# An MLP's first product as three float32r products of split operands, in place of a seven-product float32 scheme

## The chip, the cores and the metric

The kernel runs on one core of a Trainium2 chip. The metric is the device time of one execution in microseconds. The core has five engines that run side by side and wait for each other by semaphores: TensorE (PE in the profile; its weight loads are listed apart as PEld), VectorE (DVE), ScalarE (ACT), GpSimd (POOL) and SyncE (SP), which issues the transfers.

## The reference

An mLSTM cell is followed by an MLP with exact Gelu. The cell is a recurrence over 768 steps, for 4 batches and 8 heads of width 40. Its output, 3072 tokens by 320, is the MLP's input.

```python
for t in range(S):                                   # S = 768
    m_new = np.maximum(f_gate[:, :, t] + m, i_gate[:, :, t])
    f_stab = np.exp(f_gate[:, :, t] + m - m_new)
    i_stab = np.exp(i_gate[:, :, t] - m_new)
    C = f_stab * C + i_stab * (v k^T)                # cut: written with einsum
    n = f_stab * n + i_stab * k
    y[:, :, t] = sigmoid(o_gate) * (C q) / max(|n . q|, 1)
...
x = attn_out.transpose(0, 2, 1, 3).reshape(B * S, H * D)   # 3072 x 320
h = x @ w_in                                         # Up:   320 -> 2048
g = 0.5 * h * (1.0 + erf(h * inv_sqrt2))             # Gelu
return (g @ w_out).astype(np.float32)                # Down: 2048 -> 320
```

The weights w_in and w_out come as 64-bit floats; the kernel turns them into float32 on the chip.

## The kernel before

The sequence is cut into six chunks of 128 steps. In a chunk the four batches give 512 tokens (TG = 512), and the work has three parts: the cell in its chunked form (scores, carried state, values), Up with Gelu, and Down. The cell's work for the next chunk is woven into Down of the present one. The order of all steps is written as strings of letters, such as DOWN below: T is the turning (transposing) of k and q, W the weights exp(a - M), S the scores, C the carried state, V the values, Y the finish of the cell's output, X its turning, F a step of Down, M the masking of a loaded tile, G the output gate, Z a sum of weights.

```python
DOWN = """
    M0 Z M1 T0 W0 F F T1 W1 Z G3 Z F S0 Z S1 C0 M2 Z C1 G1 G0 M3 V0 Y0 Z V1 W2 Z F F T2 W3 F T3 F G2 Z Y1 S2 S3 C2
    V2 C3 Y2 V3 F F Y3 X0 F F X1 X2 F F X3 F"""
```

Up of the first chunk is a plain float32 product. For chunks two to six the kernel cuts the 320 rows of x into two blocks of 128 and a rest of 64. On the two blocks it uses a scheme of seven block products where the plain way has eight, with sums of weight blocks (in_sums, made once) and of x blocks (x_sums, made in every chunk). The rest of 64 rows is done as half-row products: two of them lie on the two halves of the array.

```python
def sum_x():                                         # once per chunk, on VectorE
    (b11, b12), (b21, b22) = x_blocks()
    t1, t2, t4 = x_sums
    for to, x, y in ((t1, b12, b11), (t2, b22, t1), (b12, b22, b12), (t4, b21, t2)):
        nc.vector.tensor_tensor(out=to, in0=x, in1=y, op=OP.subtract)

def summed_up(g, sums_too):
    ...
    def product(to, lhs, rhs, f0, first, last):
        for j in range(2):                           # 128 x 128 weights, 256 columns of x
            nc.tensor.matmul(to[:, j, :], lhs[:, (f0 + j) * P:(f0 + j + 1) * P], rhs, ...)      # L597

    def products(f0, to_sum):
        ...
        product(c11, a11, b11, f0, True, False)
        nc.scalar.copy(out=blk[1][1], in_=c11)                                                  # L606
        product(c12, s2, t2, f0, True, True)
        nc.vector.tensor_tensor(out=blk[0][0], in0=c12, in1=blk[1][1], op=OP.add)               # L608
        product(c21, s1, t1, f0, True, True)
        nc.vector.tensor_tensor(out=blk[0][1], in0=c21, in1=blk[0][0], op=OP.add)               # L610
        product(c22, s3, t3, f0, True, False)
        nc.vector.tensor_tensor(out=blk[1][0], in0=c22, in1=blk[0][0], op=OP.add)               # L612
        ...                                          # sums of hidden blocks for Down
        product(c11, a12, b21, f0, False, False)
        product(c12, s4, b22, f0, True, False)
        product(c21, a22, t4, f0, True, False)

    def rest(f0, pair, h):
        for j in range(2):
            for e in range(2):                       # e: half of the array's rows
                nc.tensor.matmul(pair[e][:, j, :], w_rest[halves[e], ...], xT[halves[e], NX, ...], ...)  # L626

    for group in ((0, 2), (4, 6)):
        sets = [products(f, group[0]) for f in group]
        ...                                          # rest for each half of the tokens
        # Gelu of c11 from PSUM (L637); the other three: add in VectorE (L639), then Gelu (L640)
    hidden_sums(g, HF - 4, HF)
```

Down uses a seven-product scheme as well (the F steps, L682), with sums of the hidden blocks (hidden_sums) and of w_out (weight_sum). Neither is changed.

The buffers that the change touches: q, k and v have four each, the mask tile Mb two and the weights W four; w_in and the sums lie in tiles of their own.

```python
qb = [const.tile([P, H, DP], F32, name=f"qb{n}") for n in range(NLD)]      # NLD = 4; kb, vb likewise
...
Mb[n] = wts.tile([P, H, L], F32, name="Mb", tag="Mb", bufs=NM)             # NM = 2
...
W[n] = wts.tile([P, H, L], F32, name="W", tag="W")                         # 4 buffers
...
# turn_y, the turning of the cell's output:
nc.scalar.copy(out=xT[:, :, t], in_=px)
if self.c > 0:
    load(n + NLD)                                    # q, k, v, o_gate of the batch four ahead
```

Of the kernel before, what the change touches and what calls it, by code (L numbers as in the profile page):

```python
# [9 lines left out]
F32 = mybir.dt.float32  # L10
BF16 = mybir.dt.bfloat16
# [4 lines left out]
P = 128  # L16

I23 = 2.0 ** 23

# [8 lines left out]
    K K J T0 W0 O6 M2 O7 A J W1 S0 C0 K J T1 L7 U U K Z K V0 T2 A M3 J J G1 S1 K W2 W3 K C1 Z A S2 Z V1 G2 J Y0 J K  # L28
    C2 Z T3 J K Y1 U U J S3 Z V2 C3 K J K K J J F K F F F Z J K J X0 K K J F F F Z J F K G3 Y2 F J K V3 J K F K X1 J
    J F F F F K Z X2 B8 J F Y3 X3 B9 F"""  # L30
DOWN = """
    M0 Z M1 T0 W0 F F T1 W1 Z G3 Z F S0 Z S1 C0 M2 Z C1 G1 G0 M3 V0 Y0 Z V1 W2 Z F F T2 W3 F T3 F G2 Z Y1 S2 S3 C2
    V2 C3 Y2 V3 F F Y3 X0 F F X1 X2 F F X3 F"""
# [3 lines left out]
def kernel(  # L37
# [32 lines left out]
    NM = 2  # L70
    NB = 4
    WP = 512
    assert S % L == 0 and 3 * BH <= P and DFF % (4 * WP) == 0 and DM == NX * P + R and DM <= WP and D <= DP and NLD == B == 4

    const = ctx.enter_context(tc.tile_pool(name="const", bufs=1))
    wts = ctx.enter_context(tc.tile_pool(name="wts", bufs=B))
# [14 lines left out]

    w_in = const.tile([P, NX, 2, DFF // 2], F32, name="w_in")
    w_rest = const.tile([P, DFF // 2], F32, name="w_rest")
# [4 lines left out]
    xT = const.tile([P, NX + 1, TG], F32, name="xT")  # L98
# [5 lines left out]
    qb = [const.tile([P, H, DP], F32, name=f"qb{n}") for n in range(NLD)]  # L104
    kb = [const.tile([P, H, DP], F32, name=f"kb{n}") for n in range(NLD)]
    vb = [const.tile([P, H, D1], F32, name=f"vb{n}") for n in range(NLD)]

    ob = [const.tile([P, DM + R], F32, name=f"ob{n}") for n in range(NLD)]
# [7 lines left out]
    def out_of(n):  # L116
        return ob[n % NLD][:, 0:DM].rearrange("p (h d) -> p h d", d=D)

    def load(n, first=0, end=4):

        if n >= NCH * B:
            return
        c, b = divmod(n, B)
        for src, dst in ((q, qb), (k, kb), (v, vb), (o_gate, None))[first:end]:
            nc.sync.dma_start(out=dst[n % NLD][:, :, 0:D] if dst else out_of(n),
                              in_=src[b, :, c * L:(c + 1) * L, :].rearrange("h p d -> p h d"))

    Mb, W = {}, {}

    def load_M(n):  # L130

        if n >= NCH * B:
            return
        c, b = divmod(n, B)
        Mb[n] = wts.tile([P, H, L], F32, name="Mb", tag="Mb", bufs=NM)
        nc.sync.dma_start(out=Mb[n].rearrange("p h l -> p (h l)"),
                      in_=M_d[c - 1, b * H:(b + 1) * H, :].rearrange("h l -> (h l)").unsqueeze(0).to_broadcast([P, H * L]))
# [3 lines left out]
    for t in kb[0:B] + qb[0:B]:  # L141
        nc.gpsimd.memset(t[:, :, D:DP], 0.0)
    for t in vb[0:B]:
        nc.gpsimd.memset(t[:, :, D:D1], 1.0)
# [19 lines left out]
    M_left = gates.tile([BH, 2, L], F32, name="M_left")  # L164
# [85 lines left out]
    w_cols = lambda e, f, n: slice(DFF * e + 2 * f, DFF * e + 2 * (f + n))  # L250
    for f in range(0, DFF // 2, WP // 2):
        for x in range(NX):
            pieces.append(([w_src["in"][x * P:(x + 1) * P, w_cols(e, f, WP // 2)] for e in range(2)],
                           w_in[:, x, :, f:f + WP // 2]))
        if f % WP == 0:
            pieces.append(([w_src["in"][NX * P:DM, w_cols(e, f, WP)] for e in range(2)], w_rest[:, f:f + WP]))
    n_in = len(pieces)
# [34 lines left out]
    def conv_two(i):  # L292

        if i < len(pieces):
# [5 lines left out]
            if len(dst.shape) == 3:  # L300
                s, p = [t.rearrange("p (e f) -> p e f", e=2) for t in (s, p)]
# [20 lines left out]
    class Cell:  # L322


        def __init__(self, c):
# [3 lines left out]
            self.qT, self.kT, self.vw, self.far, self.hs = {}, {}, {}, {}, {}  # L329
# [7 lines left out]
        def weights(self, b):  # L337

            n = self.c * B + b
            W[n] = wts.tile([P, H, L], F32, name="W", tag="W")  # L340
            if self.c > 0:
                M_n = Mb.pop(n)
# [17 lines left out]
            if self.c > 0 and not 2 * B <= n + NM < 2 * B + NM:  # L360
                load_M(n + NM)

        def gate(self, b):
            o = ob[(self.c * B + b) % NLD][:, 0:DM]
            nc.scalar.activation(out=o, in_=o, func=AF.Sigmoid)

        def turn(self, b):
            n = self.c * B + b
            for src, store, name in ((kb, self.kT, "kT"), (qb, self.qT, "qT")):
                pt = ps_tr.tile([P, NP, L], F32, name="pt", tag="tr")  # L370
                unread(pt[:, 0, :])
                for p in range(NP):
                    nc.tensor.transpose(pt[:, p, :], src[n % NLD][:, 2 * p:2 * p + 2, :].rearrange("p h d -> p (h d)"),  # L373
# [6 lines left out]
        def weigh_values(self, b):  # L380
            vw = self.vw[b] = two.tile([P, H, D1], F32, name="vw", tag="vw")
            self.engine.tensor_tensor(out=vw, in0=vb[(self.c * B + b) % NLD],
# [17 lines left out]
        def carry(self, b):  # L400
# [9 lines left out]
            if c + 1 < NCH:  # L410
                vw = self.vw.pop(b)
                for p in range(NP):
                    for hip in range(2):
                        nc.tensor.matmul(pc[halves[hip], p, :], kb[n % NLD][:, 2 * p + hip, :], vw[:, 2 * p + hip, :],  # L414
                                         start=True, stop=True)
            if c > 0:
# [4 lines left out]
                self.far[b] = two.tile([P, H, D1], F32, name="far", tag="far")  # L421
# [12 lines left out]

        def values(self, b):
# [6 lines left out]
            for h in range(H):  # L442
                for r in halves:
                    nc.tensor.matmul(ph[r, h, :], Pm[:, h, r], vb[n % NLD][:, h, :], start=True, stop=True)  # L444
# [3 lines left out]
            hs = self.hs[b] = two.tile([P, H, D1], F32, name="hs", tag="hs")  # L448
            nc.vector.tensor_tensor(out=hs, in0=ph, in1=self.far.pop(b), op=OP.add)

        def finish(self, b):
            n, hs = self.c * B + b, self.hs.pop(b)
            ys, y = ob[n % NLD], out_of(n)
            self.engine.tensor_tensor(out=y, in0=hs[:, :, 0:D], in1=y, op=OP.mult)
            den = two.tile([P, H], F32, name="den", tag="den")
# [4 lines left out]
            nc.vector.tensor_copy(out=ys[:, DM:DM + R], in_=ys[:, DM - R:DM])  # L460

        def turn_y(self, b):
# [6 lines left out]
            for k in range(NX + 1):  # L469
                nc.tensor.transpose(px[:, k, :], ob[n % NLD][:, k * P:(k + 1) * P], ident)  # L470
            nc.scalar.copy(out=xT[:, :, t], in_=px)  # L471
            if self.c > 0:
                load(n + NLD)
            if self.c > 0 and b == B - 1:
                sum_x()
# [12 lines left out]
    w_sums, in_sums, x_sums = [], [], []  # L488
    T = {1: lambda j: w_sums[0][:, j, :], 2: lambda j: w_sums[1][:, j, :], 3: Bm[0][1]}

    def sums_begin():

        gate_ctx.close()
        pool = ctx.enter_context(tc.tile_pool(name="sums_of", bufs=1))
        w_sums.extend(pool.tile([P, HF, HD], F32, name=f"w_sums{n}") for n in range(2))
        in_sums.extend(pool.tile([P, DFF // 2], F32, name=f"in_sums{n}") for n in range(3))
        x_sums.extend(pool.tile([P, HT], F32, name=f"x_sums{n}") for n in range(3))
# [31 lines left out]
    def up_step(g, sets):  # L529

        banks = []
        for k, (i0, i1, t0, t1) in sets:
            banks.append([ps_mm.tile([P, i1 - i0, t1 - t0], F32, name="pu", tag="ab"[k % 2]) for e in range(2)])
            for e in range(2):

                for i in range(i0, i1):
                    for x in range(NX):
                        nc.tensor.matmul(banks[-1][e][:, i - i0, :], w_in[:, x, e, i * P:(i + 1) * P], xT[:, x, t0:t1],  # L538
                                         start=(x == 0 and i == i0), stop=False, skip_group_check=True)
        for pu, (_, (i0, i1, t0, t1)) in zip(banks, sets):  # L540
            for i in range(i0, i1):
                for e in range(2):
                    r = halves[e]
                    nc.tensor.matmul(pu[e][:, i - i0, :], w_rest[r, i * P:(i + 1) * P], xT[r, NX, t0:t1], start=False,  # L544
                                     stop=(i + 1 == i1), skip_group_check=True)
# [26 lines left out]
    def in_sum(i):  # L572
        f, (a11, a12), (a21, a22) = slice(WP * (i // 4), WP * (i // 4 + 1)), *[[w_in[:, x, e, :] for x in range(NX)]
                                                                               for e in range(2)]
        s1, s2, s4 = in_sums
        to, x, y, op = ((s1, a21, a22, OP.add), (s2, s1, a11, OP.subtract), (a21, a11, a21, OP.subtract),
                        (s4, a12, s2, OP.subtract))[i % 4]
        nc.vector.tensor_tensor(out=to[:, f], in0=x[:, f], in1=y[:, f], op=op)

    def x_blocks():  # L580
        return [[xT[:, x, HT * h:HT * (h + 1)] for h in range(2)] for x in range(NX)]

    def sum_x():
        (b11, b12), (b21, b22) = x_blocks()
        t1, t2, t4 = x_sums
        for to, x, y in ((t1, b12, b11), (t2, b22, t1), (b12, b22, b12), (t4, b21, t2)):
            nc.vector.tensor_tensor(out=to, in0=x, in1=y, op=OP.subtract)

    def summed_up(g, sums_too):
        (a11, s3), (a12, a22) = [[w_in[:, x, e, :] for e in range(2)] for x in range(NX)]  # L590
        s1, s2, s4 = in_sums
        (b11, t3), (b21, b22) = x_blocks()
        t1, t2, t4 = x_sums
        def product(to, lhs, rhs, f0, first, last):

            for j in range(2):
                nc.tensor.matmul(to[:, j, :], lhs[:, (f0 + j) * P:(f0 + j + 1) * P], rhs, start=(first and j == 0),  # L597
                                 stop=(last and j == 1), skip_group_check=True)

        def products(f0, to_sum):  # L600

            blk = [[g.t[:, HF * e + f0:HF * e + f0 + 2, HT * h:HT * (h + 1)] for h in range(2)] for e in range(2)]
            c11, c12, c21, c22 = [pool.tile([P, 2, HT], F32, name="pu", tag=tag)
                                  for pool, tag in ((ps_tr, "tr"), (ps_h, "h"), (ps_mm, "a"), (ps_mm, "b"))]
            product(c11, a11, b11, f0, True, False)
            nc.scalar.copy(out=blk[1][1], in_=c11)  # L606
            product(c12, s2, t2, f0, True, True)
            nc.vector.tensor_tensor(out=blk[0][0], in0=c12, in1=blk[1][1], op=OP.add)  # L608
            product(c21, s1, t1, f0, True, True)
            nc.vector.tensor_tensor(out=blk[0][1], in0=c21, in1=blk[0][0], op=OP.add)  # L610
# [188 lines left out]
```

## Time and profile before

| | |
|---|---|
| time, median of three runs | 518.1 us |
| span of the profiled execution | 515.2 us |
| span until the second chunk's Up begins | 133.2 us |
| from one Up to the next (chunks three to five) | 79.6 us |
| Down of the last chunk | 30.6 us |
| transfers | 41.6 MB, mean 81 GB/s |
| mask tile Mb, 512 KB: issue to landing, median | 3.7 us |
| q, k, v, 160 KB each: issue to landing, median | 4.0, 4.5, 4.9 us |

How to read the lines. A group line has the source line, the engine and operation, output<-input, shapes, the count, then the busy time and the mean length of one, then the idle time of the engine before them with what ended most of it. A matmul's length is its latency; matmuls overlap, so their spacing is read from the chain or from the stages. The chain is the work that ended last, followed back from the end: each line is its start, its length and what it was. A stage line has the busy time of each engine in a stretch, the number of instructions in brackets, then the granted TensorE clock, the share of the transfer engines and their GB/s.

### The profile page before, as it was taken

Reading aid. Unit: us, or ns where it says so; the run is one execution under the profiler, and the core shown is the slowest. Engines: PE = TensorE matmul, PEld = TensorE weight load, DVE = VectorE, ACT = ScalarE, POOL = GpSimd, SP = SyncE. Lnnn points to the kernel's source line nnn. Section 1 sums busy time; section 2 is a strip of 40 time slices with the busy share of each in tenths; the row PEclk is TensorE's granted clock in tenths of the full one; section 3 lists DMA queues with packets and bytes.
Section 4 is the critical chain, followed back from the end, with each engine's and each line's share of the span. In section 5 each row is a group of like instructions: output and inputs, shape, how many; then the busy total and the mean of one; then the engine's idle time right before and its main releaser. Section 6 shows DMA issues by size and latency. Waiting matters only on the chain.

```text
span 515.2 us, 10957 instructions
## 1 busy us (share of the span) xinstructions
PE 500.3 (97%) x4472; PEld 450.6 (87%) x4472; DVE 340.2 (66%) x696; ACT 255.0 (49%) x523; POOL 60.9 (12%) x98
## 2 busy tenths in 40 slices
PE   4889999999999999999999999999999999999997
PEld 3778888767888999988999988999988999988997
DVE  7789598999577887347668347678347657237621
ACT  7696999555344960152980132982123882124300
POOL 3002100000210225000145000053000021000000
PEclk9799999999999999999999999999999999999999
DMA  6999751279900254900234900124920020000001
GB/s 128 223 214 212 184 147 53 64 163 171 198 0 1 84 116 58 167 0 2 74 88 69 167 28 1 43 83 81 166 52 2 5 80 1 27 27 0 1 2 51
DMA packets 111442, 41.62 MB, mean 81 GB/s; under 512 B 101184, under 2 KB 104416, under 8 KB 111392
## 3 DMA queue, kind: packets, MB, share of 16 engines
q1 hardware_dynamic: 111392, 40.92, 37.5%
q8 instruction: 35, 0.57, 0.5%
q14 instruction: 15, 0.12, 0.1%
HBM read 36.90 MB, written 4.01 MB: 79 GB/s over the span
## 4 chain that ended last, share of the span: by engine, by line
PE 91%; ACT 4%; DVE 3%; issue 0%; DMA 0%; SPq 0%; DVEq 0%; ACTq 0%
PE po L682 30%; PE pu L597 24%; PE pu L626 7%; PE po L659 7%; PE pu L538 5%; PE ps L395 4%; PE ph L444 4%; PE pt L373 4%; PE pf L419 2%; PE pf L414 2%; PE pu L544 1%; PE px L470 1%; ACT W L359 1%; ACT pow L285 1%; ACT pow L286 1%; DVE M L194 1%
## 5 line engine op out<-in xcount | busy, mean ns | idle before, releaser
L682 PE MATMUL po<-w_out,g 128*128 128x160 f32 x640 | 91.5, 299 | 0.0
L682 PEld LDWEIGHTS po<-w_out,g 128*128 128x128 f32 x640 | 88.0, 190 | 0.3 <-DVE g L639 0.3
L597 PE MATMUL pu<-xT,w_in 128*128 128x256 f32 x240 | 58.8, 381 | 0.0
L639 DVE TENSOR_TENSOR g<-pu,g 128x512 f32<-128x512 f32 x60 | 40.5, 689 | 22.4 <-PE pu L626 21.0
L597 PEld LDWEIGHTS pu<-xT,w_in 128*128 128x128 f32 x240 | 45.0, 190 | 7.5 <-ACT g L640 1.7
L471 ACT COPY xT<-px 128x384 f32<-128x384 f32 x24 | 11.1, 480 | 77.9 <-PE px L470 77.8
L359 ACT ACTIVATE W<-Mb,aT 128x128 f32<-128x128 f32 x160 | 48.9, 391 | 0.1
L682 PE MATMUL po<-w_sums,sums 128*128 128x160 f32 x320 | 47.3, 302 | 0.0
L398 DVE TENSOR_TENSOR W<-ps,W 128x512 f32<-128x512 f32 x48 | 30.2, 683 | 23.9 <-PE ps L395 21.2
L334 POOL TENSOR_SCALAR_AFFINE_SELECT Mb<-Mb 128x1024 f32<-128x1024 f32 x20 | 22.9, 1155 | 185.3 <-DMA Mb<-M_d 131.2
L682 PEld LDWEIGHTS po<-w_sums,sums 128*128 128x128 f32 x320 | 44.0, 190 | 0.4
L606 ACT COPY g<-pu 128x512 f32<-128x512 f32 x20 | 11.6, 582 | 58.2 <-PE pu L597 58.2
L695 DVE TENSOR_TENSOR o_sb<-po,o_sb 128x320 f32<-128x320 f32 (+1 forms) x27 | 12.5, 463 | 39.4 <-PE po L682 36.2
L637 ACT ACTIVATE g<-pu 128x512 f32<-128x512 f32 x20 | 12.0, 598 | 52.7 <-PE pu L626 52.7
L597 PE MATMUL pu<-x_sums,in_sums 128*128 128x256 f32 x160 | 37.8, 379 | 0.0
L626 PE MATMUL pu<-xT,w_rest 64*128 64x256 f32 x320 | 37.2, 382 | 0.0
L640 ACT ACTIVATE g<-g 128x512 f32<-128x512 f32 x60 | 36.1, 627 | 1.9
L608 DVE TENSOR_TENSOR g<-pu,g 128x512 f32<-128x512 f32 x20 | 13.8, 692 | 34.6 <-PE pu L597 28.8
L626 PEld LDWEIGHTS pu<-xT,w_rest 64*128 64x128 f32 x320 | 30.1, 187 | 6.4 <-issue 3.3
L659 PE MATMUL po<-w_out,g 128*128 128x320 f32 x128 | 35.7, 434 | 0.0
L597 PEld LDWEIGHTS pu<-x_sums,in_sums 128*128 128x128 f32 x160 | 30.2, 190 | 4.3
L659 PEld LDWEIGHTS po<-w_out,g 128*128 128x128 f32 x128 | 23.8, 190 | 9.3
(140 smaller groups left out, 884.3 us busy)
## 6 DMA issues: line engine op xcount, KB each, us to landing
Mb<-M_d SPq DMA_DIRECT2D x20, 512.0 KB, 3.7
bits<-in_moe_w_in_dram SPq DMA_DIRECT2D x20, 256.0 KB, 4.6
bits<-in_moe_w_out_dram SPq DMA_DIRECT2D x16, 320.0 KB, 3.0
vb<-in_v_dram SPq DMA_DIRECT2D x24, 160.0 KB, 4.9
ob<-in_o_gate_dram SPq DMA_DIRECT2D x24, 160.0 KB, 4.2
qb<-in_q_dram SPq DMA_DIRECT2D x24, 160.0 KB, 4.0
kb<-in_k_dram SPq DMA_DIRECT2D x24, 160.0 KB, 4.5
out_dram<-o_sb SPq DMA_DIRECT2D x24, 160.0 KB, 3.0
```

The lines of the kernel that those rows point to most:

```text
L334: nc.gpsimd.affine_select(out=t, in_=t, compare_op=OP.is_ge, fill=1.0e30, base=0, pattern=[[0, H], [1, L]], channel_multiplier=-1)
L359: nc.scalar.activation(out=W[n][:, h, :], in_=src, func=AF.Exp, scale=-1.0, bias=aT[:, self.c, r:r + 1])
L373: nc.tensor.transpose(pt[:, p, :], src[n % NLD][:, 2 * p:2 * p + 2, :].rearrange("p h d -> p (h d)"), ident)
L395: nc.tensor.matmul(ps[hip][:, p, :], kT[r, p, :], qT[r, p, :], start=True, stop=True)
L398: nc.vector.tensor_tensor(out=w, in0=ps[hip], in1=w, op=OP.mult)
L538: nc.tensor.matmul(banks[-1][e][:, i - i0, :], w_in[:, x, e, i * P:(i + 1) * P], xT[:, x, t0:t1], start=(x == 0 and i == i0), stop=False, ...
L597: nc.tensor.matmul(to[:, j, :], lhs[:, (f0 + j) * P:(f0 + j + 1) * P], rhs, start=(first and j == 0), stop=(last and j == 1), skip_group_c ...
L626: nc.tensor.matmul(pair[e][:, j, :], w_rest[halves[e], (f0 + j) * P:(f0 + j + 1) * P], xT[halves[e], NX, HT * h:HT * (h + 1)], start=False ...
L639: nc.vector.tensor_tensor(out=blk[e][h], in0=x, in1=y, op=OP.add),
L640: nc.scalar.activation(out=blk[e][h], in_=blk[e][h], func=AF.Gelu))
L659: nc.tensor.matmul(po[b], g.t[:, f, b * L:(b + 1) * L], w_out[:, f, :], start=(f == 0), stop=(f == NF - 1))
L682: nc.tensor.matmul(bank[at][:, i, :], lhs(j, t), rhs(j), start=(first and i == 0 and j == 0), stop=(i == n - 1 and j == HF - 1), skip_grou ...
```

## The change

In chunks two to six Up's two blocks and its rest are no longer done by seven float32 products. Each operand is split into a high part of 12 bits and a remainder, and Up is the sum of three products of type float32r: high by high, low by low, and a joined weight by a joined x. The scales are chosen so that the three products give the full product, up to a factor that the Gelu's scale takes back. The point is to use fewer passes of the array and whole 512-column products, with no sums after them. VectorE no longer adds products together; Gelu reads PSUM directly.

```diff
+PART = 1.0 - 2.0 ** -13
+BASE = 1.0 + 2.0 ** -12
...
+        def split_x(self, b):                        # step R, after X
+            px, t = self.px.pop(b), slice(b * L, (b + 1) * L)
+            hi = parts["x"][:, :, t]                 # written by ScalarE in X: Copy with scale=PART
+            nc.vector.scalar_tensor_tensor(out=parts["x_lo"][:, :, t], in0=px, scalar=-1.0 / BASE, in1=hi, op0=OP.mult, op1=OP.add)
+            nc.vector.tensor_tensor(out=parts["x_all"][:, :, t], in0=px, in1=hi, op=OP.subtract)
...
+    def split_weight():                              # step Z of the front (two), the other eight in the second chunk's Up
...
+        nc.scalar.activation(out=w_hi[i], in_=w, func=AF.Copy, scale=PART * 2.0 ** -12)
+        w_lo.append(w_f(F32R, "w_in_lo"))
+        nc.vector.scalar_tensor_tensor(out=w_lo[i], in0=w_hi[i], scalar=-BASE * 2.0 ** 12, in1=w, op0=OP.mult, op1=OP.add)
+    def join_weight(i):                              # ten in every chunk
+        w_mid[i] = raw.tile([P, 2, WP // 2], F32R, name="w_in_mid", tag="pow") if i % 5 in (1, 4) else w_f(F32R, "w_mid")
+        nc.vector.tensor_tensor(out=w_mid[i], in0=w_hi[i], in1=w_lo[i], op=OP.add)
...
-    def summed_up(g, sums_too):                      # and in_sum, sum_x: all removed
+    def up(g, sums_too):
...
+        def pair(f, ahead):
+            at = [f // 2 * 5 + f % 2 * 3 + x for x in range(NX)]
+            split_to(at[1])
+            for i in at:
+                if i not in w_mid:
+                    join_weight(i)
+            pus = ...                                # four PSUM banks of 512 columns
+            ahead()
+            mid = [w_mid.pop(i) for i in at]
+            for n, (w, x) in enumerate((([w_hi[i] for i in at], parts["x"]), ([w_lo[i] for i in at], parts["x_lo"]), (mid, parts["x_all"]))):
+                for i in range(2):
+                    for e in range(2):
+                        for k in range(NX):
+                            nc.tensor.matmul(pus[i][e], w[k][:, e, i * P:(i + 1) * P], x[:, k, :], ...)
+        def rest(u, banks, order):
+            mid = w_mid.pop(5 * u + 2)
+            for i in order:
+                pu = banks[i]
+                for n, (w, x) in enumerate(((w_hi[5 * u + 2], parts["x"]), (w_lo[5 * u + 2], parts["x_lo"]), (mid, parts["x_all"]))):
+                    for e in range(2):
+                        nc.tensor.matmul(pu[e], w[halves[e], i // 2, i % 2 * P:(i % 2 + 1) * P], x[halves[e], NX, :], ...)
+        def out(i, e, pu):
+            nc.scalar.activation(out=g.t[:, HF * e + i, :], in_=pu[e], func=AF.Gelu, scale=4097.0)
+
+        b0 = pair(0, lambda: split_to(4))
+        b1 = pair(1, lambda: join_weight(2))
+        rest(0, b0 + b1, (0, 1, 2, 3))
+        split_to(6)
+        join_weight(5)
+        join_weight(6)
+        ...                                          # eight Gelus of b0 and b1
+        b2 = pair(2, lambda: split_to(9))
+        hidden_sums(g, 0, 2)
+        hidden_sums(g, 2, 4)
+        b3 = pair(3, lambda: join_weight(7))
+        for step in sums_too:                        # second chunk only: two sums of w_out, 16 operations
+            step()
+        rest(1, b2 + b3, (2, 3, 0, 1))
+        ...                                          # eight Gelus of b2 and b3
+        hidden_sums(g, HF - 2, HF)
+        hidden_sums(g, HF - 4, HF - 2)
```

The parts need room. From the third chunk on, q, k and v have three buffers in place of four and are loaded three batches ahead, once the carry and the values of a batch have been computed. W is written over the mask tile that it is made from, in three buffers for both, and that tile is loaded after the values three before. Tiles of the first two chunks share their places with the high parts of the weights, the low parts go where the float32 weights were, and the first chunk's x shares with the high part of x. The order of Down changes with it: M3 and W3 come later, and R, the split of x, follows each X.

```diff
-    M0 Z M1 T0 W0 F F T1 W1 Z G3 Z F S0 Z S1 C0 M2 Z C1 G1 G0 M3 V0 Y0 Z V1 W2 Z F F T2 W3 F T3 F G2 Z Y1 S2 S3 C2
-    V2 C3 Y2 V3 F F Y3 X0 F F X1 X2 F F X3 F"""
+    M0 Z M1 T0 W0 F F T1 W1 Z G3 Z F S0 Z S1 C0 M2 Z C1 G1 G0 V0 Y0 Z V1 W2 Z M3 F F T2 F T3 W3 F G2 Z Y1 S2 S3 C2
+    V2 C3 Y2 V3 F F Y3 X0 R0 F F X1 R1 F X2 R2 F X3 R3 F"""
...
+            self.reads.append(b)                     # at the end of carry and of values
+            if self.c > 1 and self.reads.count(b) == 2:
+                load(self.c * B + b + NQ, 0, 3)      # NQ = 3
...
+            if self.c > 1:
+                load_M(n + NW)                       # NW = 3, in values
```

## The prediction

> **What bounds the kernel now.** I read four views in this order: the page's shares of busy time, the chain that ended last in order of time, the busy time by stage, and the groups of instructions kept apart by shape. The first two lines below are from the page. PE is busy in 97% of the span, and the chain runs through PE for 91% of it.
>
> ```profile
> PE 500.3 (97%) x4472; PEld 450.6 (87%) x4472; DVE 340.2 (66%) x696; ACT 255.0 (49%) x523; POOL 60.9 (12%) x98
> ...
> PE 91%; ACT 4%; DVE 3%; issue 0%; DMA 0%; SPq 0%; DVEq 0%; ACTq 0%
> ```
>
> The chain in order of time (start, length, what) shows the shape of one chunk. These lines are the third chunk's Up and the first piece of its Down:
>
> ```profile
> 212.77 12.09 PE pu L597 x56
> 224.86 3.65 PE pu L626 x32
> 228.51 12.28 PE pu L597 x56
> 240.79 3.65 PE pu L626 x32
> 244.45 1.02 PE pt L373 x8
> ```
>
> The reader is to see that one Up is four pieces of PE alone, 12.09 + 3.65 + 12.28 + 3.65 = 31.67 us, each starting where the one before ends. The other four Ups show the same lengths to 0.01 us, so the five Ups of chunks two to six hold 5 x 31.67 = 158.4 us. The stages say the same. In this answer the columns are the stretch, its length, then busy time of PE, weight loads, DVE, ACT and POOL. The first row is that Up, the second the Down and attention work after it:
>
> ```profile
> 212.77:244.45 31.68, 31.68 (x177) 26.91 (x177) 18.69 (x29) 10.53 (x18) 0.00 (x0) 1.00 0.18 31
> 244.45:292.35 47.90, 47.90 (x589) 47.22 (x590) 30.77 (x60) 25.17 (x58) 14.44 (x20) 1.00 0.47 94
> ```
>
> PE has no gap in either at full granted clock (1.00), while DVE has 13 us and ACT 21 us to spare in an Up. So a microsecond less of PE work in Up is a microsecond less of span, as long as DVE, ACT and the loads keep their work inside the shorter stage. The unit costs come from the groups by shape (busy us, then mean ns of one):
>
> ```profile
> L597 PE MATMUL pu<-xT,w_in 128*128 128x256 f32 x240 | 58.8, 381 | 0.0
> L626 PE MATMUL pu<-xT,w_rest 64*128 64x256 f32 x320 | 37.2, 382 | 0.0
> L639 DVE TENSOR_TENSOR g<-pu,g 128x512 f32<-128x512 f32 x60 | 40.5, 689 | 22.4 <-PE pu L626 21.0
> L637 ACT ACTIVATE g<-pu 128x512 f32<-128x512 f32 x20 | 12.0, 598 | 52.7 <-PE pu L626 52.7
> ```
>
> The mean of a matmul is its latency, and matmuls overlap, so I don't multiply by it. Spacing comes from the chain: 12.09 us / 56 records = 0.216 us. The program issues 28 such matmuls in that piece (two sets of seven products of two), so each float32 matmul leaves two records and costs 0.432 us for 256 columns. The 64-row products cost 3.65 / 32 = 0.114 us a record: the two halves of the array run side by side.
>
> **What the Trainium skill says.** The page "FP8 and Floating Point Precision", section "TensorE Precision Notes", says that true FP32 takes four passes through the array, and that there is a reduced form which reads four-byte values and keeps fewer bits. The trace agrees with the first: 0.432 us for 256 columns. "TensorE: Matmul & The Clock Gate", section "Back-to-back issue gap", gives 518 cycles, about 216 ns, for one warm pass of 512 columns. Four passes of 256 by its rule would be 4 x 262 cycles = 437 ns, against 432 measured. No row of this trace has a float32r matmul; that one is a single pass is an estimate from these two pages. The same page, section "Weight-path perf modes", says that fast weight load is off for FP32. The trace has weight loads running at one per 0.114 us without a gap (3.65 us for 32). "ScalarE: Activation LUTs", section "Table sets: the hidden batching unit", says copy is in every set, so the new scaled copies between Gelus should bring no table load; in the trace the plain copies of an Up cause none of their own, and the scaled form isn't there to see.
>
> **The change part by part.**
>
> Removed from PE, per Up: 56 seven-product matmuls of 256 columns, 56 x 0.432 = 24.2 us, and 32 half-row ones in 64 records, 64 x 0.114 = 7.3 us. Together with boundaries it is the 31.67 us above.
>
> Added to PE, per Up: each of four pairs does 3 products x 2 x 2 x 2 = 24 matmuls of 512 columns, 96 in all, at an estimated 0.216 us: 20.7 us. The rest is 2 x 4 x 3 x 2 = 48 half-row matmuls. Before, each half-row record was 0.114 us apart with two in flight, and a 512-column single pass streams as long as a 256-column record, so 48 x 0.114 = 5.5 us. Sum 26.2 us, saving 31.67 - 26.2 = 5.5 us per Up, **27.3 us over five**. Seven eighths of four passes is 3.5 against 3, and the narrow part goes from four to three: that is all of the gain.
>
> DVE, per Up: out go 12 adds that build the seven-product results (L608, L610, L612) and 12 of L639, 24 x 0.69 = 16.5 us. In come ten joins of weights, every chunk, 128x512 each, 10 x 0.69 = 6.9 us; the hidden sums stay, now as four groups of three, 12 x 0.69 = 8.2 us. DVE in an Up is then 15.1 us of 26.2: slack grows. Outside, the x sums (4 x 0.42 = 1.7 us) give way to eight operations on 128x384, by the 0.49 us of 128x320 about 0.55 us each, 4.4 us per chunk, in Down where DVE is busy 30.8 of 47.9 us. Hidden.
>
> ACT, per Up: 16 Gelus before (4 L637, 12 L640) and 16 after, at 0.6 us 9.6 us; four copies of 0.58 us go. Hidden. The first pair of banks is needed again when rest ends 2.7 us after it starts; ACT frees the first two after 0.7 + 2 x 0.6 = 1.9 us and the next two at 3.1 us, needed at 3.6 us. No wait.
>
> The second chunk has more: eight weight splits inside it (eight ACT of 0.6 us, eight DVE of 0.69 us = 5.5 us) and weight sums 16 x 0.32 = 5.1 us. DVE then has 15.1 + 5.5 + 5.1 = 25.7 us in 26.2 us. By order: joins 3 and 4 end about 5 us in, join 2 waits for pair 0's third product at 5.2 us; splits and joins 5 and 6 end by 11.8 us, before pair 2 needs them at 13.1 + 3.5 us. Then ACT's eight Gelus end at 15.9 us, three splits follow at 18.4 us, six hidden sums at 22.5 us, joins 8 and 9 at 23.9 us, but pair 3 wants them at 18.2 + 3.5 = 21.7 us. I put **2.2 us lost once** here.
>
> Moved: in the front, eight weight sums (8 x 0.69 = 5.5 us of DVE) go and two splits (1.4 us) and the x splits come. Near zero; the chain is PE's there by then. The q, k and v buffers of later chunks go from four to three, so the fourth batch's loads start only after the first batch's values, and the mask tile of the fourth likewise. From the end of values 0 to turn 3 PE has values 1 (0.9 us), three Down steps (4.5 and 2.2 us) and turn 2 (0.9 us) = 8.5 us. A mask load is issued in about 0.4 us, q in 0.4, k in 0.5; k lands a median 4.5 us after issue, so at about 5.8 us. It fits by under 3 us; q has taken up to 7.0 us to land in places, so I allow **2 us in all** for this and small waits.
>
> Sum: 518.1 - 27.3 + 2.2 + 2 = 495.0. I lean a little toward the plain reading, because the order of steps in Down was moved to give these loads room, and predict **494 us**.
>
> **The rivals.** (a) A float32r matmul costs more than one pass, say two cycles a column or an unhidden weight load. For it: nothing in the profile shows that type. At two passes Up would be 41.5 + 10.9 us and the kernel about 622 us. A load of 0.1 us exposed on each of 96 + 24 matmuls would be 12 us per Up, about 551 us. Against: the loads of float32 are hidden now at closer spacing, and three products would be pointless otherwise. (b) DVE becomes the bound through joins and splits. For it: the second chunk is full, and a join waits for a buffer with everything behind it in order. Against: later chunks have 11 us free. If a join stalled each Up by 2 us: 503 us. (c) Fewer buffers put DMA on the path: the mask or q/k lands late in four Downs by 2 to 3 us each: 490.8 + 2.2 + 8 to 12, so 501 to 505 us. Against: 5.8 against 8.5 us above. (d) The half-row products don't run side by side in this type: 5.2 us more per Up, which eats the gain, about 520 us. Against: float32 ones do.
>
> **Range and chances.** If every term holds with no waits it is 490.8 us; a little better if Up's boundaries shrink, 487 us. Rivals b and c together reach 504 us. So 487 to 504 us for 8 in 10. Two per cent of 518.1 is 10.4 us, so faster means under 507.7 us; only a or d, or several waits at once, break it: 0.89 faster, 0.06 within, 0.05 slower.
>
> **What would show it.** Up as one solid block of about 26 us with one record per matmul, 0.216 us apart, and half-row ones at about 0.11 us; the second chunk's Up some 2 us longer with a DVE release in its second half; Down still 47.9 us; turn 3 not waiting on a load. The prediction is wrong if records are further apart, if the half-row products stand one after another, if Down grows, or if weight loads wait for joins in chunks three to six.

## The result and the profile after

The changed kernel takes 502.96 us, the kernel before 517.62 us on the same chip: a ratio of 0.9723 with a 95% interval of 0.9707 to 0.974. It lies inside the predicted range, at its upper end, and the gain of 14.7 us is about three fifths of the 24 us foreseen. The trace says where the rest stayed.

First the page of the changed kernel, the same two lines as before. PE is still busy in 97% of a span of 501.2 us. The chain names DVE for 6% where it named it for 3%: about 10 us of that lie in the two places dealt with below, the other 20 in the opening, before PE's first long block.

```profile
PE 484.8 (97%) x4312; PEld 425.6 (85%) x4312; DVE 312.3 (62%) x663; ACT 244.0 (49%) x513; POOL 64.4 (13%) x98
...
PE 86%; DVE 6%; ACT 5%; DMA 1%; issue 1%; SPq 0%; DVEq 0%
```

The chain in order of time, again at the third chunk's Up (start, length, what):

```profile
211.42 11.17 PE pu L666 x48
222.59 2.98 PE pu L677 x24
225.57 11.38 PE pu L666 x48
236.94 2.99 PE pu L677 x24
```

The shape is as foreseen: four pieces of PE with nothing between them, and one record for each float32r matmul (48 where the program issues 48). But the sum is 28.5 us, not 26.2. In the first piece a matmul comes every 11.17 / 48 = 0.233 us, not every 0.216. The stages, with the columns as before, show that nothing but PE sets the Up, and that Down kept its length to 0.01 us:

```profile
211.42:239.93 28.51, 28.51 (x145) 22.01 (x145) 10.69 (x17) 6.08 (x12) 0.00 (x0) 1.00 0.04 12
239.93:287.84 47.91, 47.91 (x589) 47.23 (x590) 31.91 (x64) 26.50 (x60) 15.22 (x20) 1.00 0.58 107
```

The span falls by 515.2 - 501.2 = 14.0 us, and the chain's times add up to it. The Ups of chunks three to six last 28.5 us each where they lasted 31.68 (4 x 3.17 = 12.7 us less), the second chunk's 28.96 (134.55 to 163.51, 2.7 us less). The second chunk's Up begins at 134.55 us where it began at 133.19 (1.4 us more). Everything else is equal: the Downs, and the last 33.9 us.

So there are two gaps to explain: 2.3 us in each of five Ups, and the 1.4 us in the front. Four smaller points of the prediction (the second chunk's late joins, the loads, the half-row products, table loads) have their own lines below.

### The profile page after: what moved, and what is told of

Same layout as the page of the kernel before. It is cut to its first block, busy times and chain, and to the rows that moved or that the text cites. A ratio compares the mean times of both kernels' runs of the same rounds, so it can differ in the third digit from the quotient of the medians.

```text
span 501.2 us, 10573 instructions
## 1 busy us (share of the span) xinstructions
PE 484.8 (97%) x4312; PEld 425.6 (85%) x4312; DVE 312.3 (62%) x663; ACT 244.0 (49%) x513; POOL 64.4 (13%) x98
## 4 chain that ended last, share of the span: by engine, by line
PE 86%; DVE 6%; ACT 5%; DMA 1%; issue 1%; SPq 0%; DVEq 0%
PE po L738 31%; PE pu L666 21%; PE po L715 7%; PE pu L677 6%; PE ps L414 4%; PE pu L611 4%; PE ph L471 4%; PE pt L392 4%; PE pf L438 2%; PE pf L433 2%; PE px L506 1%; ACT W L378 1%; PE pu L617 1%; DMA bits<-in_moe_w_in_dram 1%; ACT g L681 1%
## 5 line engine op out<-in xcount | busy, mean ns | idle before, releaser
L681 ACT ACTIVATE g<-pu 128x512 f32<-128x512 f32 x80 | 40.8, 614 | 108.2 <-PE pu L677 108.0
L378 ACT ACTIVATE W<-W,aT 128x128 f32<-128x128 f32 x160 | 48.9, 392 | 0.1
L666 PE MATMUL pu<-x_hi,w_in_hi 128*128 128x512 f32 x160 | 41.4, 401 | 0.0
L666 PE MATMUL pu<-x_lo,w_in_lo 128*128 128x512 f32 x160 | 40.6, 395 | 0.0
L352 POOL TENSOR_SCALAR_AFFINE_SELECT W<-W 128x1024 f32<-128x1024 f32 x20 | 22.1, 1112 | 135.3 <-ACT o_sb L720 69.3
L666 PEld LDWEIGHTS pu<-x_hi,w_in_hi 128*128 128x128 f32 x160 | 29.4, 188 | 8.2 <-ACT g L681 1.9
L666 PEld LDWEIGHTS pu<-x_lo,w_in_lo 128*128 128x128 f32 x160 | 30.1, 188 | 7.2
L666 PE MATMUL pu<-x_all,w_in_mid 128*128 128x512 f32 x80 | 31.7, 396 | 0.1
L666 PE MATMUL pu<-x_all,w_mid 128*128 128x512 f32 x80 | 31.7, 396 | 0.0
L611 PE MATMUL pu<-first_x,w_in 128*128 128x256 f32 x128 | 28.8, 381 | 0.5 <-DVE W L417 0.5
```

Source lines behind the costliest of these rows:

```text
L352: nc.gpsimd.affine_select(out=t, in_=t, compare_op=OP.is_ge, fill=1.0e30, base=0, pattern=[[0, H], [1, L]], channel_multiplier=-1)
L378: nc.scalar.activation(out=W[n][:, h, :], in_=src, func=AF.Exp, scale=-1.0, bias=aT[:, self.c, r:r + 1])
L611: nc.tensor.matmul(banks[-1][e][:, i - i0, :], in_tile(i, x)[:, e, i % 2 * P:(i % 2 + 1) * P], first_x[:, x, t0:t1], start=(x == 0 and i = ...
L666: nc.tensor.matmul(pus[i][e], w[k][:, e, i * P:(i + 1) * P], x[:, k, :], start=(n == 0 and k == 0), stop=False, skip_group_check=True)
L681: nc.scalar.activation(out=g.t[:, HF * e + i, :], in_=pu[e], func=AF.Gelu, scale=4097.0)
```

## The experiments

### Why is a float32r matmul 0.233 us apart and not 0.216?

Theories: (1) two matmuls in a row that add into the same PSUM bank hold each other up; (2) the four-byte weight load beside the stream slows it; (3) a fixed cost per matmul; (4) a slower pace per column of this type; (5) the clock is held back a little under one-pass products, though the granted clock reads 1.00. The trace already speaks against a sixth, that DVE or ACT disturb PE at SBUF: in the third product of three of the four pairs of that Up, where neither engine works at all, the records are 231 to 238 ns apart as elsewhere.

**The order of a pair's matmuls** (theory 1):

```diff
-                for i in range(2):
-                    for e in range(2):
-                        for k in range(NX):
+                for k in range(NX):
+                    for i in range(2):
+                        for e in range(2):
```

> Only the order of the 24 matmuls of a pair changes: two successive ones no longer add into the same PSUM bank. In the changed kernel 512-column matmuls stand 231 to 238 ns apart (median 232) where 216 was foreseen. Bank theory (adding twice in a row into one bank costs the 16 ns): spacing falls to 216 ns, each Up from 28.5 to about 26.9 us, the span by 8 us to about 493 us. Weight-load theory (a four-byte weight load slows the moving stream beside it), fixed-cost theory, column-rate theory and power theory: spacing stays at 232 ns, span 501 us.

Measured: the first piece of the third chunk's Up 11.17 us and the whole Up 28.5 us, as in the changed kernel; span 501.8 us. Theory 1 falls.

**x set to zero** (theory 5). The high part of x and x_lo get the scale zero, and x_all is multiplied by the zero high part, so the products are all zero while the number and shape of the instructions stay:

```diff
-            nc.scalar.activation(out=parts["x"][:, :, t], in_=px, func=AF.Copy, scale=PART)
+            nc.scalar.activation(out=parts["x"][:, :, t], in_=px, func=AF.Copy, scale=0.0)
...                                                  # x_lo: scalar=0.0; x_all: op=OP.mult in place of OP.subtract
```

> All parts of x are zero (scales set to zero), so the products are left out in value while every instruction stays. Power theory (the clock is held back a little under dense one-pass products): spacing falls to 216 ns in Up, Up to about 27 us, span to about 493 us. All the other theories: nothing moves, 232 ns and 501 us.

Measured: 11.17 us for the piece, span 501.9 us. What the data are doesn't matter, so theory 5 falls as far as it rests on them; and the bfloat16 run below sends as many one-pass products through the array, as close together, at 216 ns.

**Half as many columns, twice as many matmuls** (theories 3 and 4):

```diff
-                            nc.tensor.matmul(pus[i][e], w[k][:, e, i * P:(i + 1) * P], x[:, k, :], ...)
+                            for h in range(2):
+                                c = slice(HT * h, HT * (h + 1))
+                                nc.tensor.matmul(pus[i][e][:, c], w[k][:, e, i * P:(i + 1) * P], x[:, k, c], ...)
```

> Each 512-column matmul of the pairs becomes two of 256 columns with the same weights, 192 an Up in place of 96. If the excess is per matmul (a weight load beside the stream, or a fixed cost): spacing about 107 + 18 = 125 ns, Up 28.5 + 96 x 0.018 = about 30.2 us, span up by about 9 us. If the excess is a slower rate per column (232/512 = 0.453 ns): spacing 116 ns, Up and span unchanged at 28.5 and 501 us. If the type itself is slow under 512 columns, more than either.

The chain of this run at the third chunk's Up:

```profile
211.45 11.49 PE pu L668 x96
222.94 2.99 PE pu L679 x23
225.93 11.68 PE pu L668 x96
```

Twice the matmuls cost 0.32 us a piece. 11.49 / 96 = 119.7 ns for 256 columns. That lies between the 125 of a fixed cost and the 116 of a pure pace: the line through 256 and 512 columns is 0.441 ns a column and 6.7 ns for each matmul with its weight load.

**384 columns.** In the pairs all matmuls but the first of each bank stream three of the four batches; the fourth's products are mostly left out:

```diff
+                            m = TG if n == 0 and k == 0 else TG - P
-                            nc.tensor.matmul(pus[i][e], w[k][:, e, i * P:(i + 1) * P], x[:, k, :], ...)
+                            nc.tensor.matmul(pus[i][e][:, 0:m], w[k][:, e, i * P:(i + 1) * P], x[:, k, 0:m], ...)
```

> In the pairs, all matmuls but the first of each bank stream 384 columns (the fourth batch's products are mostly left out). So far 512 columns take 233.3 ns and 256 take 119.7. A pace per column with a small fixed cost (0.444 ns a column and 6 ns) gives 176.5 ns; a cost of the weight load that grows with the share of the stream it covers, about 177 to 178; a fixed 18 ns per matmul, 180 ns.

Measured: the piece takes 8.93 us with 8 matmuls of 512 columns and 40 of 384: (8.93 - 8 x 0.2327) / 40 = 176.7 ns. The line above gives 176.2. Theory 3 alone (180) falls, and so does a pure pace (384 x 232.7 / 512 = 174.5 ns): most of the cost goes with the columns, about 7 ns with each matmul. A weight load that covers more of a short stream was expected at 177 to 178, too near to be parted by this, so the next run asks for it alone.

**Half the weight columns** (theory 2), with the upper half of the results left out:

```diff
+                            m = P if n == 0 and k == 0 else R
-                            nc.tensor.matmul(pus[i][e], w[k][:, e, i * P:(i + 1) * P], x[:, k, :], ...)
+                            nc.tensor.matmul(pus[i][e][0:m], w[k][:, e, i * P:i * P + m], x[:, k, :], ...)
```

> In the pairs, all matmuls but the first of each bank load 64 weight columns in place of 128 (the upper half of the results is left out); 512 columns of x stream past them as before. If the four-byte weight load slows the stream beside it, the excess over 216 ns halves: about 225 ns apart, Up about 27.7 us. If the four-byte moving operand itself sets the pace, or a fixed cost of the type: 233 ns apart, Up 28.5 us, span 501 us.

Measured: 11.11 us a piece, so (11.11 - 8 x 0.2327) / 40 = 231.2 ns for a matmul with 64 weight columns against 232.7 with 128. The load was not halved, though: its record is 134 ns long here, 188 ns in the changed kernel and 98 ns in the bfloat16 run below. If the excess over bfloat16, 232.7 - 215.8 = 17 ns, came with the load's length beyond 98 ns, these 54 ns less would have taken 10 ns away. It was 1.5 ns. So theory 2 falls as the main cause, as far as it goes by the length of the load; what a load may cost whatever its length is part of the 7 ns.

**bfloat16 parts.** Every part is bfloat16, which leaves out the precision of the split; number and shape of the matmuls are the same:

```diff
-F32R = mybir.dt.float32r
+F32R = mybir.dt.bfloat16
```

> All parts are bfloat16 in place of float32r, so this leaves out the precision of the split; the number and shape of the matmuls stay. Weight-load theory (four-byte weights): spacing falls to about 216 ns, Up to about 27 us, span to about 493 us. Fixed cost per matmul or power: stays near 232 ns. Reading four bytes a column of the moving operand as the cause would also give 216 ns, so this run parts the type from the matmul, and the half-width run parts weights from moving operand.

The chain and the stage of this run, third chunk's Up:

```profile
210.41 10.36 PE pu L666 x48
220.77 2.70 PE pu L677 x24
223.47 10.47 PE pu L666 x48
233.94 2.70 PE pu L677 x24
```

```profile
210.41:236.64 26.23, 26.23 (x146) 11.39 (x144) 8.02 (x17) 5.94 (x12) 0.00 (x0) 1.00 0.04 13
```

10.36 / 48 = 0.216 us, and the Up lasts 26.23 us: the predicted 26.2 to the last digit, for a type that the change doesn't use. The half-row pieces are shorter as well, 2.70 against 2.98 us. So the count of matmuls, the two halves side by side and the hidden weight loads were judged rightly, and the one pass of 512 columns too; what was missing is that a float32r matmul of 512 columns takes 8% longer than a bfloat16 one (232.7 against 215.8 ns). The run makes both operands narrower at once, so it shows that the type is the cause and not which operand.

How the 17 ns divide can only be estimated, since bfloat16 ran at one length. In the changed kernel's chain, float32 records of 160 columns stand 4.35 / 32 = 0.136 us apart and those of 320 columns 8.62 / 32 = 0.269 us. With two passes to a record, as the prediction reads them, that is 0.417 ns a column and 2.4 ns besides, which would give 216 ns for one pass of 512 columns, as bfloat16 has. Beside this, float32r's 0.441 ns a column is 6% slower, some 12 of the 17 ns, and some 4 ns more go with each matmul.

**The columns of x in another order.** Two columns from the first half of the tokens, two from the second, and so on, the results written back in the same order:

```diff
+                            two_by = lambda t: t.rearrange("p (h c two) -> p c h two", h=2, two=2)
-                            nc.tensor.matmul(pus[i][e], w[k][:, e, i * P:(i + 1) * P], x[:, k, :], ...)
+                            nc.tensor.matmul(two_by(pus[i][e]), w[k][:, e, i * P:(i + 1) * P], two_by(x[:, k, :]), ...)
```

> In the pairs the 512 columns of x are streamed in another order, two from the first half, two from the second, with the results put back in place: same data, same work. If the 6% slower pace a column of float32r comes from how four-byte columns are fetched one after another, the spacing of 233 ns moves, up or down. If it belongs to the type in the array whatever the order of fetching, it stays at 233 ns and the span at 501 us.

```profile
221.47 15.71 PE pu L667 x48
237.19 2.98 PE pu L678 x24
240.17 16.30 PE pu L667 x48
```

15.71 / 48 = 0.327 us a matmul (0.340 in the second piece), 40% more, with the same data and the same work; the half-row products, whose order wasn't changed, keep their 2.98 us. So the pace depends on the order in which columns are read or written. The run changed both at once, so it doesn't say which. That the excess in the plain order has the same cause is not shown, and bfloat16 wasn't run in this order, so neither is it that the type matters here. Why a float32r column is slower stays open.

| kernel | columns | apart |
|---|---|---|
| changed kernel | 512 | 232.7 ns |
| other order of matmuls | 512 | 232.7 ns |
| x zero | 512 | 232.7 ns |
| half the weight columns | 512 | 231.2 ns |
| 384 columns | 384 | 176.7 ns |
| 256 columns | 256 | 119.7 ns |
| bfloat16 | 512 | 215.8 ns |
| columns two by two | 512 | 327 ns |

### Why does the second chunk's Up begin 1.4 us later?

The kernel before has PE alone in its chain just before that Up. Its first long block of PE, and the end of the front:

```profile
57.57 7.17 PE pu L538 x32
...
131.03 2.16 PE po L659 x8
133.19 12.09 PE pu L597 x56
```

The changed kernel's chain runs through ACT and DVE there:

```profile
57.73 7.17 PE pu L611 x32
...
128.74 0.50 ACT x_hi L516
...
129.27 0.56 DVE x_lo L524
129.82 0.47 DVE x_all L525
130.29 0.40 DVE ob L484
...
131.24 0.50 DVE ob L489
...
131.88 0.52 PE px L506 x3
132.40 2.15 PE po L715 x8
134.55 11.17 PE pu L666 x48
```

R2, the split of the third x (L524), stands in DVE's queue before Y3, the finish of the fourth output (L484 to L489). DVE idles 1.62 us there until ACT's copy is done, and Y3 starts only after R2. The fourth output's turning (L506) waits for Y3. The test moves one word of the front's order:

```diff
-    J R1 F F F F K X2 B8 J R2 F Y3 Z Z X3 R3 B9 B10 F"""
+    J R1 F F F F K X2 B8 J Y3 R2 F Z Z X3 R3 B9 B10 F"""
```

> One word of the front's order is moved: the last cell output's finish (Y3) comes before the split of the third x (R2), so VectorE doesn't wait for ScalarE's copy in front of it. Theory: R2 held Y3 back by 2 us on VectorE and with it the last transposes, which is the 1.4 us by which the second chunk's Up begins later than before (134.55 against 133.19 us). Then that Up begins at 133.2 to 133.5 us and the time falls by 1.0 to 1.4 us, to about 501.8. Rival: the front is late because VectorE has more work in all (two weight splits and eight x operations), then nothing moves.

Measured: 502.42 us, ratio 0.971 (0.9697 to 0.9723) to the kernel before, and the Up begins at 134.34 us: at first sight a miss. But the opening, up to the first long block of PE, varies from run to run: that block begins at 57.57 us in the kernel before, at 57.73 in the changed kernel, and in the experiments anywhere from 57.31 to 58.76. The distance from that block to the second chunk's Up is what the order sets. In both runs of the changed kernel and in the eight experiments with its front it is 76.82 or 76.83 us. In the kernel before it is 133.19 - 57.57 = 75.62 us, and here, from 58.72 to 134.34, 75.62 us again, as in both runs of the next kernel. So R2 before Y3 cost 1.20 us, the move gives all of it back, and the other 0.16 us of the 1.36 is the opening's variation. The chain of this run shows PE alone:

```profile
58.72 7.17 PE pu L611 x32
...
129.70 2.16 PE po L715 x8
131.85 0.33 PE px L506 x3
132.18 2.15 PE po L715 x8
134.34 11.18 PE pu L666 x48
```

### The second chunk's Up

That Up lasts 28.96 us, 0.45 more than the others. The changed kernel's chain in it:

```profile
152.81 0.69 DVE w_in_lo L564
153.50 0.61 DVE sums L598
...
156.76 0.60 DVE g L600
157.37 0.60 DVE w_mid L570
157.97 0.61 DVE w_in_mid L570
...
158.62 1.90 PE pu L666 x7
```

This is the chain that the prediction foresaw: splits, six hidden sums, then joins 8 and 9, and PE's third product of pair 3 behind them. Only its end shows on PE. The next kernel adds to the move above that the second group of hidden sums follows the joins:

```diff
         hidden_sums(g, 0, 2)
-        hidden_sums(g, 2, 4)
         b3 = pair(3, lambda: join_weight(7))
+        hidden_sums(g, 2, 4)
```

> As the run before it, and the second group of hidden sums follows the joins of pair 3 in place of preceding them. Theory: in the second chunk VectorE's chain of splits, sums and joins holds pair 3's third product back by 0.4 us, so this gives 0.4 us more: about 501.4 us. Rival: the joins wait for buffers anyway, then the same as the run before it.

Measured: 501.61 us, ratio 0.9697 (0.9683 to 0.9711). Its second chunk's Up runs from 133.85 to 162.40 us, 28.55 us: 0.42 less than the 28.97 of the run before it, and DVE is gone from the chain there. To see the 1.6 us directly, the changed kernel and this one ran once more side by side:

> The changed kernel once more beside the next run on one chip: 502.5 to 503.5 us.

> By the stages of its trace this order gains 1.20 us in the front and 0.42 us in the second chunk's Up, 1.6 us in all, against the changed kernel: 501 to 501.8 us beside 502.5 to 503.5. Rival: the opening's varying start (57.3 to 58.7 us in the traces so far) hides it, within 0.5 us of each other.

Measured: 503.62 us (502.62 to 503.93) and 501.64 us (501.23 to 502.27), with ratios to the kernel before of 0.9728 (0.9713 to 0.9744) and 0.9698 (0.9683 to 0.9712). Neither the intervals nor the times of the runs overlap. This is the fastest kernel of the study; the trace puts its gain at 1.6 us.

### Were the three buffers near the path?

Down didn't move, so the loads fit. By how much? In the third chunk's Down k for turn 3 lands at 259.9 us and PE turns it at 262.0. The test issues these loads one batch later, all but those of a chunk's last batch, which stay where they were:

```diff
             if self.c > 1 and self.reads.count(b) == 2:
-                load(self.c * B + b + NQ, 0, 3)
+                for d in ([1] if b else []) + ([0] if b == B - 1 else []):
+                    load(self.c * B + b - d + NQ, 0, 3)
```

> In chunks three to six the loads of q, k and v for the batch three ahead are issued one batch later: after the next batch's reads in place of after its own. In the changed kernel k for turn 3 of the third chunk's Down lands at 259.9 us and PE turns it at 262.0, a margin of 2.1 us. Theory (the three buffers fit, by a margin of about 2 us, which is why Down stayed at 47.9 us): the loads now stand behind another 512 KB mask and land about 4.5 us later, so PE waits some 2 to 3 us at turn 3 in each of the four Downs: Down about 50.5 us, span 510 us or so. Rival (the loads were never near the path): nothing moves, 501 us.

The chain of this run in the same Down, and the line of PE's waits that is new:

```profile
256.70 7.24 DMA kb<-in_k_dram
263.94 0.14 issue
264.07 1.06 PE pt L392 x8
```

```profile
PE pt L392 <- DMA kb<-in_k_dram: 2.2, 2, 1.4
```

k now lands at 263.9 us and PE's turning hangs on it. From the second chunk's Up to the fourth's it is 134.25 to 290.10 = 155.85 us, where the changed kernel has 287.84 - 134.55 = 153.29: 2.6 us lost in two Downs. The other two lose 0.2 us at most. So the direction was right, and the size was not: 2 to 3 us were expected in each of four Downs, and 1.4 and 1.1 us came in the first two and next to nothing in the others, 2.4 us of span in all (503.6 against 501.2 us). Why the last two hardly lose is not shown. The margin is real and small: k lands about 4 us later, and PE waits.

## Why the prediction was right, and which term was off

**Up is PE's alone, and PE's saving is the span's.** Right: 28.51 us of PE in 28.51 us, and 3.17 us less per Up came through to the span in full.

**The size of Up: 26.2 us foreseen, 28.5 measured.** This is the term of the sum that failed: "96 in all, at an estimated 0.216 us", and the 48 half-row ones at 0.114. They came at 0.233 and, with the piece's start, at 2.98 / 24 = 0.124: (96 x 0.017) + (48 x 0.010) = 2.1 us more than foreseen, and 0.2 us more at the start of the second pair block (11.38 against 11.17 us). Over five Ups that is 11.5 us of 27.3. The step behind it carried the time of a pass from one type to another, with nothing in the trace that had the new type. The run with bfloat16 shows that it holds for that type and not for float32r. Rival (a), a slower type, was given two passes or an exposed load of 0.1 us; what came was 17 ns a matmul, a twelfth of the one and a sixth of the other, between the plain reading and the rival.

**The half-row products side by side.** Right; rival (d) is out. Two records start 2 to 5 ns apart.

**DVE's and ACT's work in Up.** Right: DVE is busy 10.7 us there (six of the twelve hidden sums run after the Up), ACT 6.1 us, no wait of PE for either in chunks three to six. The scaled copies brought no table load: the line of the Gelus has five in all, as before.

**The second chunk, 2.2 us foreseen, 0.45 measured.** The chain was named rightly. DVE needed what was foreseen: joins 8 and 9 end 24.0 us after the Up's beginning, 23.9 foreseen. But PE came to the third product of pair 3 only at 158.06 us, 23.5 us after the beginning, where 21.7 was foreseen. So PE's own slowness hid the rest. In bfloat16, where PE is faster but the joins are shorter too (0.42 against 0.69 us), the same Up lost 0.74 us against its neighbours (26.97 against 26.23 us).

**The front, "near zero; the chain is PE's there by then", 1.2 us measured.** Wrong in its reason. The sum of DVE's work hardly changed, as said, but the order did: one instruction that waits for another engine held up five that PE needed.

**The allowance of 2 us for loads and small waits.** None came; the estimate that k lands 5.8 us after the values was near (it landed at 259.9 us, 6.3 us after the mask's load was issued at 253.6), and the run with later loads shows how little was left.

Together: 495.0 foreseen by the sum; 11.5 us for the type, 1.2 for the front's order and 0.2 for the opening, less 1.8 for the second chunk and 2 for the waits, gives 504.1 us: the 518.1 us it started from less the 14.0 us that the trace shows. The timed runs, 502.96 beside 517.62, fell by 14.7. The 494 that I named, a little under my own sum, leaned the wrong way.

That 502.96 us lies inside 487 to 504 is in part luck. The upper end was set by rivals (b) and (c), and neither came; the 11.5 us came from a term that had no range, and 3.8 us of allowances that weren't needed made up for some of it. The upper end was also mis-added: by the figures given, (b) and (c) together make 490.8 + 2.2 + 10 + 8 = 511 us or more, and not 504.

## What to carry to other kernels

When a change brings in a type or a form that the trace doesn't hold, give its unit time a range of its own: 8% on one matmul, with the starts of its pieces, was two fifths of the predicted gain here. Before adding an instruction to an in-order queue, ask not how long it is but what it waits for and who stands behind it; moving one word gave back 1.2 us. And to compare fronts whose opening varies, measure from the first solid block, not from zero.

## What the runs showed of the hardware

- A float32r matmul of 256, 384 and 512 columns stands 119.7, 176.7 and 232.7 ns from the next: about 0.44 ns a column and 7 ns. A bfloat16 one of 512 columns stands 215.8 ns apart. Neither zero data, nor another order of banks, nor half the weight columns changes the 232.7 ns by more than 1.5 ns.
- The record of a weight load is 188 ns long for 128 columns of float32r, 134 ns for 64 columns and 98 ns for 128 columns of bfloat16. With 256-column matmuls the 128-column loads overlap: PE starts a matmul every 119.7 ns.
- Streaming the same 512 columns two by two from two halves, with the results written in that order, took 327 to 340 ns.
- Splitting a 512-column float32r matmul in two of 256 with the same weights cost 2 x 119.7 - 232.7 = 6.7 ns.
